# Three normed tiles of a linear-attention and SwiGLU kernel go from TensorE's transpose to the DMA's, and their gain to ScalarE

## Chip, cores and metric

The kernel runs on one core of a Trainium2 chip. The metric is device time in microseconds of one execution, lower is better. One further execution was profiled; its trace gives the span (first to last instruction of the program), and its own time contains a little more than the span.

## What is computed

The reference is an RWKV-6 recurrence followed by a gated feed-forward layer. Sizes: batch B = 4, H = 8 heads, S = 768 steps, D = 48 per head, so the model width is 384; the feed-forward width is 1536. All inputs are float32.

```python
for t in range(S):
    cur = einsum('bhd,bhe->bhde', u * k[t], v[t])
    y[t] = einsum('bhd,bhde->bhe', r[t], state + cur)
    state = w[t][..., None] * state + einsum('bhd,bhe->bhde', k[t], v[t])
x  = y.transpose(0, 2, 1, 3).reshape(3072, 384)
xn = x / sqrt(mean(x * x, -1) + 1e-6) * rms_g
g, val = xn @ w_gate, xn @ w_val
out = (g * sigmoid(g) * val) @ w_out
```

## The kernel before

The 768 steps are cut into six superblocks of 128. In names such as `xn_pe.2.0` the first number is the superblock and the second the batch; for `gate_mm`, `val_mm`, `silu` and `h_mul` the second number is one of twelve slices of the feed-forward width.

The recurrence of one superblock and batch is done in closed form. `ln` takes the logarithm of the decay, `cs_mm` sums it along the block on TensorE, `cs_add` adds the block's own step on VectorE, `exp_r` and `exp_k` take exponentials on ScalarE, and `r_mul` (VectorE) and `k_mul` (GpSimd from superblock 2 on) scale r and k by them into one tile `rk`. `rk_tr` transposes `rk`, by DMA from superblock 2 on. `q_mm` makes the scores, `q_mask_e`, `q_copy_o` and `q_mask_o` mask them, `y_mm` applies them and the old state, `st_mm` and `st_new` make the new state. `bonus_mul`, `bonus_sum` and `bonus_v` make the term with u, which `x_add` adds.

The norm of one tile of 128 rows and 384 columns: `x_sq` sums the squares on ScalarE, `x_rstd` makes the reciprocal root on GpSimd, `xn_mul` (L585) scales the rows on ScalarE into a bfloat16 tile `xn`, of which there are three buffers. The feed-forward matmuls need this tile with the 384 columns on partitions, in `xnt`, one tile of 128 x 3 x 512 for the four batches of a superblock, in two buffers. There are two ways to it:

- `xn_pe` (L596): three 128x128 transposes on TensorE into one PSUM bank; then `xn_out` (L607) multiplies by the norm's weights `gT` on VectorE while it copies from PSUM into `xnt`. Superblocks 0 to 3 go this way.
- `xn_tr` (L590): one DMA transpose issued by SP, from `xn` straight into `xnt`; then `xn_gain` multiplies `xnt` in place, one third of the columns of all four batches at a time. Superblocks 4 and 5 go this way.

```python
nc.sync.dma_start_transpose(xnt[n][:, :, j * L:(j + 1) * L], bank.pop(("xn", n, j)))
```

Then come 24 groups of matmuls a superblock (`gate_mm` and `val_mm`, three matmuls of 512 columns each), `silu` on ScalarE, `h_mul` on VectorE, and per batch `o_mm` (twelve matmuls), `o_out` (copy from PSUM, on VectorE or ScalarE) and `out_dma`.

The order is written out by hand. The string `ORDER` lists 1086 steps over all engines, and each step puts its instructions at the end of its engines' queues. An engine does its own instructions in that order and waits only for the data and the buffers that the next one needs. All loads, DMA transposes and stores of the output stand in SP's queue; the loads of the weights are issued by GpSimd. The feed-forward part of one superblock and the recurrence of the next are interleaved in `ORDER`.

PSUM has eight banks in three rings: "a" (names ps_au, ps_av) and "b" (ps_bu, ps_bv) are used by `cs_mm`, `cs_add`, `gate_mm` and `val_mm`, "q" (ps_qu, ps_qv, ps_qx, ps_qz) by the rest, `xn_pe` and `o_mm` among them. A helper looks ahead in `ORDER` for the last use of each bank and hands out the one that came free first.

Of the kernel before, what the change touches and what calls it, by code (L numbers as in the profile page):

```python
# [74 lines left out]
exp_k.3.3 cs_mm.3.2 xn_out.2.3 o_mm.1.2 load_r.3.2 k_mul.3.1 w_tot.3.3 rk_tr.3.0 r_mul.3.3 cs_add.3.2 out_dma.1.0
xn_out.2.1 load_v.3.0 exp_r.3.2 gate_mm.2.5 exp_k.3.2 r_mul.3.2 w_tot.3.2 val_mm.2.0 gate_mm.2.0 bonus_mul.3.0
bonus_mul.3.2 k_mul.3.2 o_out.1.3 bonus_sum.3.0 silu.2.5 rk_tr.3.1 load_k.3.3 o_out.1.2 q_mm.3.0 silu.2.0 q_mask_e.3.0
val_mm.2.1 bonus_v.3.0 h_mul.2.0 gate_mm.2.1 load_w.4.1 load_v.3.1 load_k.4.3 st_mm.3.2 k_mul.3.3 q_copy_o.3.0
silu.2.1 rk_tr.3.2 load_v.4.0 rk_tr.3.3 val_mm.2.5 gate_mm.2.11 load_k.4.0 bonus_sum.3.1 cast_v.3.0 out_dma.1.1
# [10 lines left out]
o_out.2.0 x_rstd.3.2 xn_mul.3.2 w_tot.4.0 ln.4.2 exp_r.4.1 load_r.5.1 x_rstd.3.3 k_mul.4.0 xn_out.3.0 load_r.4.3  # L90
out_dma.1.3 bonus_sum.4.1 xn_pe.3.1 xn_out.3.1 ln.4.3 exp_k.4.1 bonus_mul.4.2 xn_mul.3.3 r_mul.4.1 k_mul.4.1 w_tot.4.1
out_dma.2.0 o_mm.2.1 cs_mm.4.2 xn_pe.3.3 bonus_mul.4.0 cast_v.4.1 xn_pe.3.2 o_out.2.1 cs_mm.4.3 bonus_sum.4.2
rk_tr.4.0 xn_out.3.3 cs_add.4.3 load_k.5.3 o_mm.2.3 exp_r.4.3 xn_out.3.2 cs_add.4.2 bonus_mul.4.3 r_mul.4.3 w_tot.4.3
exp_k.4.3 exp_r.4.2 rk_tr.4.1 o_out.2.3 exp_k.4.2 load_v.4.2 val_mm.3.1 gate_mm.3.6 bonus_sum.4.0 k_mul.4.3 r_mul.4.2
st_mm.4.0 w_tot.4.2 load_r.5.3 load_k.5.0 val_mm.3.0 o_out.2.2 silu.3.6 st_new.4.0 k_mul.4.2 gate_mm.3.1 q_mm.4.0
cast_v.4.2 out_dma.2.2 bonus_sum.4.3 silu.3.1 gate_mm.3.0 q_copy_o.4.0 silu.3.0 h_mul.3.1 q_copy_o.4.1 gate_mm.3.3
val_mm.3.6 gate_mm.3.8 rk_tr.4.3 q_mask_e.4.0 h_mul.3.0 h_mul.3.6 st_mm.4.1 bonus_v.4.0 q_mask_e.4.1 q_mask_o.4.0
load_r.5.0 bonus_v.4.2 rk_tr.4.2 load_v.5.1 q_mask_o.4.1 bonus_v.4.1 silu.3.3 gate_mm.3.4 val_mm.3.4 val_mm.3.3
y_mm.4.0 silu.3.4 st_new.4.1 gate_mm.3.9 h_mul.3.4 load_v.4.3 load_r.5.2 load_k.5.1 silu.3.8 x_add.4.0 val_mm.3.8
# [5 lines left out]
load_v.5.3 x_sq.4.2 xn_tr.4.0 h_mul.3.11 x_sq.4.3 xn_tr.4.1 val_mm.3.5 st_mm.4.3 h_mul.3.5 x_rstd.4.2 cs_mm.5.1
cs_add.5.1 ln.5.2 xn_mul.4.2 x_rstd.4.3 o_mm.3.2 o_out.3.2 cs_mm.5.2 xn_tr.4.2 exp_k.5.1 cs_add.5.2 exp_r.5.1 o_mm.3.0
xn_mul.4.3 r_mul.5.1 ln.5.3 ln.5.0 xn_tr.4.3 cs_mm.5.0 st_new.4.3 exp_r.5.2 cast_v.5.3 exp_k.5.2 o_mm.3.1 out_dma.3.2
cs_add.5.0 out_dma.2.3 r_mul.5.2 exp_r.5.0 cs_mm.5.3 r_mul.5.0 st_mm.4.2 exp_k.5.0 cs_add.5.3 exp_r.5.3 o_mm.3.3
bonus_mul.5.1 xn_gain.4.0 xn_gain.4.2 xn_gain.4.1 k_mul.5.0 r_mul.5.3 exp_k.5.3 o_out.3.1 out_dma.2.1 o_out.3.0
gate_mm.4.0 val_mm.4.1 gate_mm.4.1 val_mm.4.0 bonus_sum.5.1 st_new.4.2 k_mul.5.1 k_mul.5.3 silu.4.0 load_v.5.0  # L110
rk_tr.5.0 silu.4.1 h_mul.4.0 gate_mm.4.3 gate_mm.4.2 rk_tr.5.1 silu.4.3 val_mm.4.2 bonus_sum.5.0 k_mul.5.2 gate_mm.4.4
silu.4.2 bonus_v.5.1 o_out.3.3 cast_v.5.0 h_mul.4.1 val_mm.4.3 q_mm.5.0 gate_mm.4.6 h_mul.4.2 bonus_mul.5.2 h_mul.4.3
silu.4.4 q_copy_o.5.0 q_mask_o.5.0 gate_mm.4.5 out_dma.3.1 q_mask_e.5.0 y_mm.5.0 silu.4.6 q_copy_o.5.1 bonus_v.5.0
rk_tr.5.2 load_v.5.2 silu.4.5 rk_tr.5.3 x_add.5.0 val_mm.4.4 q_mask_o.5.1 gate_mm.4.8 val_mm.4.5 q_mask_e.5.1
h_mul.4.4 bonus_sum.5.2 q_mm.5.2 q_copy_o.5.2 gate_mm.4.10 val_mm.4.6 bonus_v.5.3 cast_v.5.2 silu.4.8 h_mul.4.5
q_copy_o.5.3 cast_v.5.1 q_mask_e.5.3 q_mask_e.5.2 q_mask_o.5.2 silu.4.10 h_mul.4.6 gate_mm.4.7 x_sq.5.0 y_mm.5.1
q_mask_o.5.3 silu.4.7 bonus_v.5.2 x_rstd.5.0 x_add.5.1 val_mm.4.10 y_mm.5.3 val_mm.4.7 y_mm.5.2 gate_mm.4.11 x_add.5.3
x_sq.5.1 h_mul.4.10 x_sq.5.3 x_rstd.5.1 h_mul.4.7 xn_mul.5.1 val_mm.4.8 out_dma.3.3 gate_mm.4.9 silu.4.11 x_rstd.5.3
xn_mul.5.3 xn_tr.5.1 h_mul.4.8 xn_mul.5.0 val_mm.4.11 xn_tr.5.3 x_add.5.2 x_sq.5.2 x_rstd.5.2 val_mm.4.9 silu.4.9
# [5 lines left out]
val_mm.5.9 gate_mm.5.10 silu.5.9 h_mul.5.6 h_mul.5.9 val_mm.5.8 silu.5.10 val_mm.5.10 gate_mm.5.11 h_mul.5.8
h_mul.5.10 val_mm.5.11 silu.5.11 h_mul.5.11 o_mm.5.0 o_mm.5.3 o_out.5.3 o_mm.5.1 out_dma.5.3 o_out.5.1 o_out.5.0
out_dma.5.0 o_mm.5.2 out_dma.5.1 o_mm.5.4 o_out.5.2 out_dma.5.2 o_out.5.4 out_dma.5.4
# [597 lines left out]
```

## Time and profile before

| what | value |
|---|---|
| three runs | 200.31, 201.06, 201.94 us (median 201.06) |
| profiled execution | 200.28 us |
| its span | 198.6 us |
| TensorE matmul busy | 191.9 us (97%) |
| VectorE busy | 151.4 us (76%) |
| ScalarE busy | 137.3 us (69%) |
| GpSimd busy | 125.2 us (63%) |
| DMA traffic | 32.41 MB, mean 163 GB/s |
| granted TensorE clock | full in all 40 slices of the page |

Engines are named PE (TensorE matmul), PEld (its weight loads), DVE (VectorE), ACT (ScalarE), POOL (GpSimd) and SP (the queue that issues DMAs). In rows of the timeline the first number is the start in us from the beginning of the span, the second the length, then engine, line, operation, tile written and tiles read, shapes and the count of merged instructions; brackets tell how long the engine had been idle and who ended that. L235 is a helper for all activations that need a table (`ln`, `exp_r`, `exp_k`, `silu`), so there the tile names tell the step: lw is `ln`, ps_au or ps_av written in place is `exp_r`, ek is `exp_k`, sg is `silu`. Matmul records overlap, so the step from one start to the next is the time that a matmul holds TensorE.

### The profile page before, as it was taken

The page shows a single profiled execution, that of the slowest core. Times are in us where ns is not written, and L with a number is a line of the kernel's source. Part 1 is how long each engine was busy: PE and PEld are TensorE (multiplying, and loading weights), DVE is VectorE, ACT ScalarE, POOL GpSimd, SP SyncE. Part 2 cuts the span into 40 slices and gives each one's busy share as a digit, 9 for nine tenths or more (in the row PEclk, how much of TensorE's full clock was granted, in tenths as well). Part 3 has the DMA queues.
Part 4 walks back from the last instruction along what each step waited for, and adds up shares of the span by engine and source line. Part 5 has one row for each costly group of instructions (what it writes and reads, how often), then busy time and mean ns, then how long its engine had stood idle before and what let it go on. Part 6 is the DMA issues. An engine that isn't in the chain of part 4 may idle for free.

```text
span 198.6 us, 4409 instructions
## 1 busy us (share of the span) xinstructions
PE 191.9 (97%) x1577; PEld 113.9 (57%) x1577; DVE 151.4 (76%) x290; ACT 137.3 (69%) x279; POOL 125.2 (63%) x184
## 2 busy tenths in 40 slices
PE   7979998999999999999999999999999999999994
PEld 3556574465665565665556665556655565555562
DVE  6358989989998799987889989987887973173611
ACT  4399989579979569958559959399786683164300
POOL 5378993189399687899939899867686851000000
PEclk9999999999999999999999999999999999999999
DMA  6999999999999998999899879995499012032012
GB/s 153 268 235 176 183 220 203 214 180 211 179 195 224 206 196 196 236 198 207 193 195 225 188 171 204 204 183 107 138 187 208 0 25 60 6 112 83 0 59 101
DMA packets 121566, 32.41 MB, mean 163 GB/s; under 512 B 116420, under 2 KB 120392, under 8 KB 121544
## 3 DMA queue, kind: packets, MB, share of 16 engines
q1 hardware_dynamic: 119504, 28.58, 67.3%
q0 software_dynamic: 2032, 3.54, 10.0%
q8 instruction: 12, 0.20, 0.4%
q14 instruction: 10, 0.08, 0.1%
q10 hardware_dynamic: 8, 0.00, 0.0%
HBM read 25.96 MB, written 4.72 MB: 154 GB/s over the span
## 4 chain that ended last, share of the span: by engine, by line
PE 72%; SPq 18%; DMA 6%; POOL 2%; issue 1%; ACT 0%; POOLq 0%
SPq L248 16%; PE ps_av L626 10%; PE ps_bu L626 10%; PE ps_bv L626 10%; PE ps_au L626 10%; PE ps_qv L672 7%; PE ps_qz L672 7%; PE ps_qu L672 5%; PE ps_qx L672 4%; DMA wo_sb<-in_moe_w_out_dram 4%; DMA vt<-in_v_dram 3%; SPq L261 2%; PE ps_qz L502 1%; PE ps_qx L552 1%; PE ps_av L417 1%
## 5 line engine op out<-in xcount | busy, mean ns | idle before, releaser
L672 PEld LDWEIGHTS <-ht 128*128 128x128 bf16 x300 | 28.2, 98 | 17.0 <-issue 0.5
L626 PEld LDWEIGHTS <-wg_sb 128*128 128x128 bf16 x216 | 23.1, 114 | 19.7 <-DMA wg_sb<-in_moe_w_gate_dram 0.7
L626 PEld LDWEIGHTS <-wv_sb 128*128 128x128 bf16 x216 | 22.8, 114 | 19.0 <-DMA wv_sb<-in_moe_w_val_dram 1.0
L658 DVE TENSOR_TENSOR ht<-ps_bv,sg 128x512 bf16<-128x512 f32 x35 | 24.0, 686 | 10.1 <-PE ps_bv L626 9.2
L235 ACT ACTIVATE sg<-ps_av 128x512 bf16<-128x512 f32 x37 | 22.0, 595 | 12.3 <-PE ps_av L626 12.0
L626 PE MATMUL ps_av<-xnt,wg_sb 128*128 128x512 bf16 x111 | 30.1, 380 | 0.0
L626 PE MATMUL ps_bu<-xnt,wv_sb 128*128 128x512 bf16 x111 | 30.1, 380 | 0.0
L658 DVE TENSOR_TENSOR ht<-ps_bu,sg 128x512 bf16<-128x512 f32 x37 | 25.4, 686 | 6.0 <-PE ps_bu L626 5.2
L626 PE MATMUL ps_bv<-xnt,wv_sb 128*128 128x512 bf16 x105 | 28.5, 380 | 0.6 <-DMA wv_sb<-in_moe_w_val_dram 0.5
L626 PE MATMUL ps_au<-xnt,wg_sb 128*128 128x512 bf16 x105 | 28.5, 380 | 0.2 <-DMA wg_sb<-in_moe_w_gate_dram 0.2
L235 ACT ACTIVATE sg<-ps_au 128x512 bf16<-128x512 f32 x35 | 21.0, 599 | 10.8 <-PE ps_au L626 9.0
L467 POOL TENSOR_TENSOR ruk<-rt,kt 128x384 f32<-128x384 f32 x24 | 24.1, 1003 | 6.6 <-DMA kt<-in_k_dram 4.8
L468 POOL TENSOR_TENSOR ruk<-ruk,u_bc 128x384 f32<-128x384 f32 x24 | 24.4, 1017 | 1.9
L520 POOL TENSOR_SCALAR_AFFINE_SELECT qts<-qts 128x512 bf16<-128x512 bf16 x20 | 12.9, 653 | 15.1 <-ACT qts L513 14.6
L477 POOL TENSOR_TENSOR ydiag<-vt,diag 128x384 f32<-128x384 f32 x24 | 19.9, 833 | 1.0 <-DVE rk L461 0.5
L461 POOL TENSOR_TENSOR rk<-kt,ek 128x384 bf16<-128x384 f32 x16 | 15.9, 1007 | 2.3 <-ACT ek L235 2.3
L672 PE MATMUL ps_qv<-wo_sb,ht 128*128 128x384 bf16 (+1 forms) x96 | 15.0, 306 | 0.0
L672 PE MATMUL ps_qz<-wo_sb,ht 128*128 128x384 bf16 x84 | 14.8, 326 | 0.0
L233 ACT ACT_TABLE_LOAD x10 | 12.8, 1283 | 1.8 <-PEq L709 1.6
L235 ACT ACTIVATE lw<-wt 128x384 bf16<-128x384 f32 (+1 forms) x20 | 11.1, 578 | 4.2 <-DMA wt<-in_w_dram 4.1
L472 DVE TENSOR_REDUCE diag<-ruk 128x8 f32<-128x384 f32 x24 | 12.9, 543 | 0.7 <-POOL ruk L468 0.7
L585 ACT ACTIVATE xn<-xb,rstd 128x384 bf16<-128x384 f32 x20 | 11.8, 605 | 0.8 <-POOL rstd L580 0.8
(180 smaller groups left out, 373.6 us busy)
## 6 DMA issues: line engine op xcount, KB each, us to landing
rt<-in_r_dram SPq DMA_DIRECT2D x24, 192.0 KB, 3.9
kt<-in_k_dram SPq DMA_DIRECT2D x24, 192.0 KB, 4.0
vt<-in_v_dram SPq DMA_DIRECT2D x24, 192.0 KB, 3.7
out_dram<-ob SPq DMA_DIRECT2D x23, 192.0 KB, 2.3
wt<-in_w_dram SPq DMA_DIRECT2D x16, 192.0 KB, 4.0
wt<-in_w_dram SPq DMA_DIRECT2D x4, 384.0 KB, 4.4
wo_sb<-in_moe_w_out_dram POOLq DMA_DIRECT2D x3, 384.0 KB, 7.1
wg_sb<-in_moe_w_gate_dram POOLq DMA_DIRECT2D x1, 768.0 KB, 9.8
```

The source lines that it names most:

```text
L233: nc.scalar.preload_act_table_set(table_name)
L235: return nc.scalar.activation(**kw).ins
L248: dmas["load_" + which, n, j] = nc.sync.dma_start(out=inp[which, n, j], in_=t[j, :, n * L:(n + 1) * L, :].rearrange("h t d -> t h d")).ins
L461: eng.tensor_tensor(out=rk[:, n % 2, j, 1, :, 0:D], in0=inp["k", n, j], in1=bank["cs_k", n, j][:, 0:DM].rearrange("p (h d) -> p h d", h=H) ...
L467: nc.gpsimd.tensor_tensor(out=ruk[n, j], in0=inp["r", n, j], in1=inp["k", n, j], op=ALU.mult)
L468: nc.gpsimd.tensor_tensor(out=ruk[n, j], in0=ruk[n, j], in1=u_bc, op=ALU.mult)
L472: nc.vector.tensor_reduce(out=diag[n, j].rearrange("p h o -> p (h o)"), in_=ruk[n, j], axis=mybir.AxisListType.X, op=ALU.add)
L477: nc.gpsimd.tensor_tensor(out=ydiag[n, j], in0=inp["v", n, j], in1=diag[n, j].to_broadcast([128, H, D]), op=ALU.mult)
L520: nc.gpsimd.affine_select(out=qts[n, j][:, 1], in_=qts[n, j][:, 1], compare_op=ALU.is_gt, fill=0.0, base=0, pattern=[[0, NP], [1, 128]], c ...
L626: nc.tensor.matmul(ps[:, cols], lhsT=units(ws, c, f), rhs=xnt[n][:, c, cols], start=(first and c == 0), stop=(c == KC - 1))
L658: nc.vector.tensor_tensor(out=ht[n][:, f, :], in0=bank.pop(("v", n, f)), in1=bank.pop(("sg", n, f)), op=ALU.mult)
L672: nc.tensor.matmul(ps[:, cols], lhsT=ht[n][:, f, b * L:(b + 1) * L], rhs=wo_sb[:, f, cols], start=(f == 0), stop=(f == FC - 1))
```

## The change

Three of the 24 tiles, batch 0 of superblock 2 and batches 0 and 1 of superblock 3, go from the first way to a mixture of both: `xn_tr` transposes them by DMA, and `xn_out`, for these three, multiplies the three 128x128 blocks of `xnt` in place on ScalarE, with the weight as a scale per partition. Their `xn_pe` steps go. One load is moved up by a few steps. Nothing else in the program changes.

```diff
+    XT_DMA = sel("30 20 31")
...
     def xn_out(n, j):
         if n not in xnt:
             xnt[n] = pt.tile([128, KC, TS], BF16, name="xnt")
+        if (n, j) in XT_DMA:
+            for c in range(KC):
+                t = xnt[n][:, c, j * L:(j + 1) * L]
+                nc.scalar.activation(out=t, in_=t, func=AF.Copy, scale=gT[:, c:c + 1])
+            return
         ps = bank.pop(("xt", n, j))
```

The rest is in `ORDER`. Its lines are broken anew, so the diff is given here by steps, with neighbours:

```diff
 o_mm.1.0 cs_mm.3.1
-xn_pe.2.0
 exp_r.3.0 ln.3.2
...
 load_k.3.2 load_r.3.3
+load_r.3.2 xn_tr.2.0
 xn_pe.2.1
-xn_out.2.0
 exp_r.3.3 exp_k.3.3
+xn_out.2.0
 cs_mm.3.2 xn_out.2.3 o_mm.1.2
-load_r.3.2
 k_mul.3.1 w_tot.3.3 rk_tr.3.0
...
 cast_v.3.3 val_mm.2.11 xn_mul.3.0
+xn_tr.3.0
 q_mask_e.3.2
...
 cs_mm.4.1 x_sq.3.1
-xn_pe.3.0
 x_add.3.2
...
 x_rstd.3.3 k_mul.4.0
-xn_out.3.0
 load_r.4.3 out_dma.1.3
+xn_tr.3.1
 bonus_sum.4.1
-xn_pe.3.1 xn_out.3.1
 ln.4.3 exp_k.4.1 bonus_mul.4.2 xn_mul.3.3
+xn_out.3.0
 r_mul.4.1 k_mul.4.1 w_tot.4.1 out_dma.2.0 o_mm.2.1 cs_mm.4.2 xn_pe.3.3 bonus_mul.4.0 cast_v.4.1 xn_pe.3.2 o_out.2.1
+xn_out.3.1
 cs_mm.4.3 bonus_sum.4.2
```

Three PSUM banks of ring "q" fewer are taken, so some later `o_mm` and `xn_pe` steps get another bank of that ring.

More of the change, by code (lines that the diff above doesn't have):

```diff
@@ L75 @@
[L75 to L79, printed above, removed]
@@ L90 @@
[L90 to L94, printed above, removed]
@@ L95 @@
[L95 to L99, printed above, removed]
@@ L105 @@
[L105 to L109, printed above, removed]
@@ L110 @@
[L110 to L119, printed above, removed]
@@ L125 @@
[L125 to L127 removed]
+load_r.3.0 x_sq.2.2 xn_mul.2.0 cast_v.3.2 cs_add.3.0 x_add.2.3 exp_k.3.0 x_sq.2.3 o_mm.1.0 cs_mm.3.1 exp_r.3.0 ln.3.2
+x_rstd.2.2 o_mm.1.1 st_new.2.3 load_r.3.1 out_dma.0.3 w_tot.3.0 r_mul.3.0 xn_mul.2.1 k_mul.3.0 xn_mul.2.2 cs_add.3.1
@@ new lines @@
+exp_k.3.1 xn_pe.2.2 cs_mm.3.3 x_rstd.2.3 o_out.1.0 exp_r.3.1 bonus_mul.3.1 xn_out.2.2 xn_mul.2.3 o_mm.1.3 w_tot.3.1
+xn_pe.2.3 o_out.1.1 cs_add.3.3 r_mul.3.1 load_k.3.2 load_r.3.3 load_r.3.2 xn_tr.2.0 xn_pe.2.1 exp_r.3.3 exp_k.3.3
+xn_out.2.0 cs_mm.3.2 xn_out.2.3 o_mm.1.2 k_mul.3.1 w_tot.3.3 rk_tr.3.0 r_mul.3.3 cs_add.3.2 out_dma.1.0 xn_out.2.1
+load_v.3.0 exp_r.3.2 gate_mm.2.5 exp_k.3.2 r_mul.3.2 w_tot.3.2 val_mm.2.0 gate_mm.2.0 bonus_mul.3.0 bonus_mul.3.2
+k_mul.3.2 o_out.1.3 bonus_sum.3.0 silu.2.5 rk_tr.3.1 load_k.3.3 o_out.1.2 q_mm.3.0 silu.2.0 q_mask_e.3.0 val_mm.2.1
@@ new lines @@
+x_add.3.3 cs_mm.4.0 bonus_mul.4.1 ln.4.1 cs_mm.4.1 x_sq.3.1 x_add.3.2 x_sq.3.2 cs_add.4.0 h_mul.2.8 st_new.3.3
+o_mm.2.0 x_sq.3.3 o_mm.2.2 exp_r.4.0 load_k.4.2 cs_add.4.1 exp_k.4.0 r_mul.4.0 x_rstd.3.1 xn_mul.3.1 o_out.2.0
+x_rstd.3.2 xn_mul.3.2 w_tot.4.0 ln.4.2 exp_r.4.1 load_r.5.1 x_rstd.3.3 k_mul.4.0 load_r.4.3 out_dma.1.3 xn_tr.3.1
+bonus_sum.4.1 ln.4.3 exp_k.4.1 bonus_mul.4.2 xn_mul.3.3 xn_out.3.0 r_mul.4.1 k_mul.4.1 w_tot.4.1 out_dma.2.0 o_mm.2.1
+cs_mm.4.2 xn_pe.3.3 bonus_mul.4.0 cast_v.4.1 xn_pe.3.2 o_out.2.1 xn_out.3.1 cs_mm.4.3 bonus_sum.4.2 rk_tr.4.0
@@ new lines @@
+xn_out.3.3 cs_add.4.3 load_k.5.3 o_mm.2.3 exp_r.4.3 xn_out.3.2 cs_add.4.2 bonus_mul.4.3 r_mul.4.3 w_tot.4.3 exp_k.4.3
+exp_r.4.2 rk_tr.4.1 o_out.2.3 exp_k.4.2 load_v.4.2 val_mm.3.1 gate_mm.3.6 bonus_sum.4.0 k_mul.4.3 r_mul.4.2 st_mm.4.0
+w_tot.4.2 load_r.5.3 load_k.5.0 val_mm.3.0 o_out.2.2 silu.3.6 st_new.4.0 k_mul.4.2 gate_mm.3.1 q_mm.4.0 cast_v.4.2
+out_dma.2.2 bonus_sum.4.3 silu.3.1 gate_mm.3.0 q_copy_o.4.0 silu.3.0 h_mul.3.1 q_copy_o.4.1 gate_mm.3.3 val_mm.3.6
+gate_mm.3.8 rk_tr.4.3 q_mask_e.4.0 h_mul.3.0 h_mul.3.6 st_mm.4.1 bonus_v.4.0 q_mask_e.4.1 q_mask_o.4.0 load_r.5.0
```

62 lines of the change are left out of this document (39 added, 23 removed).

## The prediction

> **What bounds the kernel now.** I read the page first for the chain that ended last, then the windows for what TensorE does along that chain, then the timeline around the six places that the change touches.
>
> ```profile
> span 198.6 us, 4409 instructions
> ...
> PE 72%; SPq 18%; DMA 6%; POOL 2%; issue 1%; ACT 0%; POOLq 0%
> ```
>
> ```profile
> 82.84:86.60 3.76, 3.76 (x32) 2.40 (x30) 3.25 (x9) 3.62 (x9) 3.51 (x6) 1.00 1.05 190
> 53.00:196.00 143.00, 142.47 (x1115) 84.18 (x1114) 108.46 (x209) 95.33 (x196) 90.23 (x132) 1.00 0.68 149
> ```
>
> The second row (columns: stretch, its length, busy time of PE, PEld, DVE, ACT, POOL, granted clock, DMA share, GB/s) is the main reading. From 53 to 196 us TensorE works 142.47 of 143.00 us at full clock. The chain is queue and DMA at the beginning and TensorE from there on. The three moved tiles all lie inside this stretch (82 to 118 us). So a TensorE instruction taken out there shortens the kernel by its own share of the stream, and anything that makes TensorE wait lengthens it. VectorE time is worth nothing in itself. The first row shows that the DMA engines are full (share 1.05, overlapping packets counted) just where the first new DMA transpose is put.
>
> **The change, part by part.** The time around the span is 200.28 - 198.6 = 1.7 us, which no part touches. The profiled run is 0.8 us below the median of 201.06, so I make the sum against 200.28 and carry it to the median.
>
> *Removed from TensorE: 9 transposes (xn_pe.2.0, 3.0 and 3.1, three each).*
>
> ```profile
> 82.66 0.33 PE L596 MATMUL ps_qx<-ident,xn 128*128 128x128 bf16 x3
> 82.83 0.49 PE L672 MATMUL ps_qu<-wo_sb,ht 128*128 128x384 bf16 x2
> ```
>
> The three transposes start at 82.66 and the next matmul at 82.83: they hold the stream for 0.17 us, though their records last 0.33, since records overlap. All three steps stand in the same dense stream, so 3 x 0.17 = 0.50 us.
>
> *Removed from VectorE: three gain products of 0.55 us each* (the kind of the 89.00 row below). It is off the chain, so zero; it only lets VectorE come earlier to its next wait.
>
> *Added to the SP queue: three DMA transposes, one of them behind load_r.3.2, which moves up.* In the SP queue nothing stands between the old and the new place of load_r.3.2, so its own move costs nothing.
>
> ```profile
> L596 PE MATMUL ps_qu<-ident,xn x18: 218/219/219, 26.0 to 116.0; 128*128 128x128 bf16 x18
> ...
> L590 SPq DMA_TRANSPOSE xnt<-xn x8: 1178/1198/1390, 133.5 to 166.0; - x8
> ...
> DMA to landing us min/median/max: 2.3/2.3/3.1
> ```
>
> ```profile
> DMA to landing us min/median/max: 2.7/3.3/3.8
> ```
>
> The first fence is tile xn, the second the landings of tile rkT (16 larger transposes, mostly in the full DMA stage). The same instruction already runs for superblocks 4 and 5: 1.2 us of SP, landing 2.3 to 3.1 us after issue where DMA is half empty; rkT's took up to 3.8 us. I take 2.3 to 3.8 as the bounds, and 3.3 as the value, for the full stage.
>
> *Superblock 2.* SP first:
>
> ```profile
> 80.84 2.00 SPq L248 DMA_DIRECT2D rt<-in_r_dram  x2
> 83.90 1.36 SPq L489 DMA_TRANSPOSE rkT<-rk  x1
> ```
>
> ```profile
> 81.19 0.60 ACT L585 ACTIVATE xn<-xb,rstd 128x384 bf16<-128x384 f32 x1
> ```
>
> SP is free at 82.84 and would wait until 83.90 for rk. xn.2.0 is ready at 81.79, so xn_tr.2.0 issues at 82.84 and holds SP to 84.04: rk_tr.3.0 comes 0.14 us later, without a reader in a hurry (its q_mm stands behind the first two matmul groups of superblock 2). The landing is at 82.84 + 2.3 to 3.8 = 85.1 to 86.6.
>
> ```profile
> 86.73 0.48 ACT L235 ACTIVATE ek<-ps_bu 128x384 f32<-128x384 f32 x1
> 89.19 0.48 ACT L235 ACTIVATE ps_av<-ps_av 128x388 f32<-128x388 f32 x1 [1.97 <-DVE ps_bv L425]
> ```
>
> xn_out.2.0 now stands on ScalarE between these two (exp_k.3.3 and exp_r.3.2), in an idle time of 1.97 us. It is three products of 128 columns in place. Their price is not in the trace; the nearest rows:
>
> ```profile
> L612 ACT ACTIVATE xnt<-xnt,gT 128x512 bf16<-128x512 bf16 x1 | 0.7, 712 | 0.0
> ```
>
> The same product on 512 columns takes 712 ns, the 384-column scaling by rstd 610 ns (114.11 row below), so about 102 ns per 128 columns and about 400 ns for 128. Two scalings in a row start 0.5 us apart and last 0.6 (111.50 row), so 0.1 overlaps: 0.3 us each, 0.9 us per tile. Bounds: 0.6 (0.2 each, half of the extrapolated price) to 1.5 (no cheaper than a 384-column one, 0.5 each). All shifted by -0.17, ScalarE reaches the step at 87.0 and is done at 87.9, at worst 88.5; exp_r.3.2 is released at 89.0. Hidden; cover left 0.5 to 1.1 us. The first matmul of superblock 2 needs all four tiles:
>
> ```profile
> 89.00 0.55 DVE L607 TENSOR_TENSOR xnt<-ps_qu,gT 128x384 bf16<-128x384 bf16 x1
> ...
> 89.70 0.81 PE L626 MATMUL ps_au<-xnt,wg_sb 128*128 128x512 bf16 x3
> ```
>
> The last VectorE tile (xn_out.2.1) ends at 89.55, 0.15 before TensorE takes it. It hangs on TensorE's transposes of 2.3 and 2.1, so it moves up with them; the gain of 0.17 survives here.
>
> The xn tiles have three buffers, and a DMA read holds one for longer than TensorE did. xn_mul.2.3 comes before xn_tr.2.0 in the order, so it can only be given a tile whose reader stands ahead of it, which is 2.2's, read by TensorE. No wait on the DMA here; if there were one, the landing at 86.1 would hold xn_mul.2.3 by about 0.9 us, for which the 1.97 us of idle time would still serve.
>
> *Superblock 3.*
>
> ```profile
> 105.01 1.54 SPq L248 DMA_DIRECT2D rt<-in_r_dram  x1
> ...
> 105.58 0.61 ACT L585 ACTIVATE xn<-xb,rstd 128x384 bf16<-128x384 f32 x1
> ...
> 106.60 0.70 SPq L261 DMA_DIRECT2D wt<-in_w_dram  x1
> ```
>
> Here SP does wait. At 105.01 it issued load_r.4.2; now xn_tr.3.0 stands first and waits for xn_mul.3.0 (105.58 + 0.61 = 106.19), then issues for 1.2 us: load_r.4.2 and all loads behind it start up to 2.3 us later. The DMA queue drains meanwhile, so they then issue faster, and I take 1.1 us for their landings.
>
> ```profile
> wt<-in_w_dram SPq DMA_DIRECT2D x16, 192.0 KB, 4.0
> ...
> wo_sb<-in_moe_w_out_dram POOLq DMA_DIRECT2D x3, 384.0 KB, 7.1
> ```
>
> ```profile
> 111.50 1.10 ACT L585 ACTIVATE xn<-xb,rstd 128x384 bf16<-128x384 f32 x2
> 112.50 0.51 ACT L235 ACTIVATE lw<-wt 128x384 bf16<-128x384 f32 x1
> ...
> 114.11 0.61 ACT L585 ACTIVATE xn<-xb,rstd 128x384 bf16<-128x384 f32 x1
> 115.70 0.48 ACT L681 COPY ob<-ps_qv 128x384 f32<-128x384 f32 x1 [0.99 <-PE ps_qv L672]
> 117.21 0.48 ACT L235 ACTIVATE ps_av<-ps_av 128x388 f32<-128x388 f32 x1 [1.03 <-DVE ps_bv L425]
> 117.60 0.48 ACT L235 ACTIVATE ek<-ps_bv 128x384 f32<-128x384 f32 x1
> ```
>
> The tightest reader is ln.4.2 on ScalarE (112.50). Its load lands at 106.60 + 4.0 + 1.1 = 111.7, in time; at 2.3 it would be 112.9, 0.6 late. The next users (POOL's product of r and k) have about as much room.
>
> xn_out.3.0 comes behind xn_mul.3.3: 114.72 - 0.17 = 114.55 to 115.45. o_out.2.1 is released by TensorE at 115.70 - 0.50 = 115.20, so it goes at 115.45, 0.25 late, and ScalarE is free for the next start 0.42 later (exp spacing 117.21 to 117.60 is 0.39). xn_out.3.1 runs from 115.87 to 116.77. exp_r.4.3 could go at 117.21 - 0.50 = 116.71 and goes at 116.77; exp_k.4.3 ends 0.39 + 0.48 later, at 117.64.
>
> ```profile
> 118.31 0.81 PE L626 MATMUL ps_bv<-xnt,wv_sb 128*128 128x512 bf16 x3
> ```
>
> val_mm.3.1 writes the bank that exp_k.4.3 reads (ps_bv), and TensorE gets there at 118.31 - 0.50 = 117.81. It has 0.17 us to spare: the two idle times of 0.99 and 1.03 us hide the two products, but barely. At 1.5 us per tile, exp_k.4.3 would end at 118.84 and TensorE would lose 1.0 us. xn_tr.3.1 issues when xn_mul.3.1 is done, at 112.0, and lands at 115.3 (114.3 to 115.8), ahead of 115.87.
>
> **Sum:** -0.50 + 0 + 0 = -0.50 us: 199.8 in the profiled execution, 200.6 on the median's scale.
>
> A rule that speaks against this stands in the Trainium skill, VectorE: DVE Perf Modes, section The three transpose paths: 390 ns for a 128x128 transpose on TensorE, 1309 ns by DMA, and a DMA transpose only where TensorE's will not do. By it the nine would free 3.5 us of TensorE (an estimate from that page); the row's 0.17 us per three decides against that price, and the DMA's longer path agrees with the landings but runs beside the chain.
>
> **The rivals.**
>
> *ScalarE gives the gain back in superblock 3 (no change).* If the load stream holds SP until 113.2 and xn_tr.3.1 takes 3.8 us, it lands at 117.0; the product ends at 117.9, exp_k.4.3 at 118.77, and val_mm.3.1 starts 0.96 us late: -0.50 + 0.96 = +0.46, 201.5. For it: only 0.17 us of room. Against: both tiles have an idle time of their own.
>
> *A slow landing blocks ScalarE's queue (slower).* xn_out waits in order, so exponentials, output copies and SiLUs queue behind it. The places are xn_out.2.0, from a landing of 5.3 us on (89.02 - 0.9 - 82.84), and xn_out.3.1, from 3.9 (115.87 - 112.0). With the 7.1 us of wo_sb's loads (the longest median): 2.0 lands at 89.94, its product ends at 90.84 instead of the 89.70 at which the group began, +1.14; 3.1 lands at 119.1, its product ends at 120.0, exp_k.4.3 at 120.9, val_mm.3.1 comes 2.6 us after its 118.31. Together +3.7 us, 204.8. For it: DMA is full here, and a wait on ScalarE hits many readers. Against: of the 24 such transposes none that the trace follows took over 3.8 us.
>
> *TensorE frees the whole record.* If each transpose cost its 219 ns, 9 x 0.22 = 1.97 us go: 199.1. For it: only the records. Against: the start of the next matmul. The 390 ns of the Trainium skill (VectorE: DVE Perf Modes, The three transpose paths) would be the far end of this case, 197.6 as an estimate.
>
> *The change does nothing:* TensorE reaches another wait 0.5 us earlier, in the second half. 201.1. Against: 0.53 us of idle in 143.
>
> **How the numbers follow.** A measurement of this kernel can tell about 1% (2 us) from no change. Forecast 0.42, gain given back 0.27, slow landing 0.21, whole record 0.07, nothing 0.03. Over 1% faster: 0.05, of the whole record's. Over 1% slower: 0.21, the slow landing's with a little of the second. Within: 0.74. The low end, 199.4, is the forecast less a part of the whole-record case and the scatter between runs; the high end, 203.0, covers the given-back case with both upper bounds and the milder part of the slow landings, and leaves the rest out.
>
> **What would show it.** Right: gate_mm.2.5 starts near 89.5, val_mm.3.1 near 117.8, TensorE stays at 99% from 53 us to its end; xn_tr lands within 3.8 us; the idle times of 1.97, 0.99 and 1.03 us shrink. Wrong: ScalarE shows a wait for DMA xnt, TensorE one before val_mm.3.1 or for ScalarE's xnt, or ln.4.2 waits for wt.

## The result, and the profile after

The changed kernel takes 202.0 us (median of 19 runs, 200.4 to 203.7), the kernel before 200.84 us beside it (19 runs). The ratio is 1.0057, 95% interval 1.0033 to 1.0081: slower by 1.2 us, where 0.5 us faster was forecast. Both lie within the 1% that I had set as the bound, but the sign is wrong and the interval leaves no doubt of it. Executions in the slower state are left out of every ratio here: two of these 19 (203.71 us each), and up to four of twelve in the runs below (e4).

The page of the changed kernel: its span, and the shares of the chain that ended last.

```profile
span 200.9 us, 4381 instructions
...
PE 58%; DMA 17%; SPq 13%; ACT 5%; POOL 2%; issue 2%; DVE 2%; ACTq 0%; POOLq 0%
```

The same stretch as in the prediction, from the windows (length, then busy time of PE, PEld, DVE, ACT, POOL, granted clock, DMA share, GB/s):

```profile
53.00:196.00 143.00, 140.05 (x1077) 82.26 (x1092) 106.94 (x206) 97.75 (x204) 90.47 (x132) 1.00 0.71 150
```

TensorE was busy 142.47 us of this stretch and now is 140.05, at the same clock; the DMA share went from 0.68 to 0.71. (There are 1077 matmul records against 1115; nine fewer are the change's, and more are missing from this trace, so the busy time falls by more than TensorE really waits.) TensorE lost time twice. The timeline around the first place:

```profile
83.38 2.74 SPq L591 DMA_TRANSPOSE xnt<-xn  x1
...
85.19 2.11 PE L678 MATMUL ps_qv<-wo_sb,ht 128*128 128x384 bf16 x12
...
87.57 0.61 ACT L586 ACTIVATE xn<-xb,rstd 128x384 bf16<-128x384 f32 x1 [2.13 <-DMA xnt<-xn]
...
88.24 0.34 PE L597 MATMUL ps_qz<-ident,xn 128*128 128x128 bf16 x3 [0.94 <-ACT xn L586]
...
89.23 0.97 ACT L605 ACTIVATE xnt<-xnt,gT 128x128 bf16<-128x128 bf16 x3
...
90.80 0.81 PE L632 MATMUL ps_au<-xnt,wg_sb 128*128 128x512 bf16 x3
```

The third row is xn_mul.2.3. It waits 2.13 us for the DMA that reads xn.2.0 (first row: issue from 83.38 on, 2.74 us of SP, landed 4.1 us after the start of the issue). TensorE comes to xn_pe.2.3 and finds no xn: 0.94 us of idle time and 0.17 of the overlap that matmul records have in a dense stream, 1.11 us.

The second place, in superblock 3:

```profile
107.74 1.30 SPq L591 DMA_TRANSPOSE xnt<-xn  x1
...
114.59 2.08 SPq L591 DMA_TRANSPOSE xnt<-xn  x1
114.74 1.00 POOL L468 TENSOR_TENSOR ruk<-rt,kt 128x384 f32<-128x384 f32 x1 [0.51 <-DMA kt<-in_k_dram]
...
116.59 0.46 ACT L687 COPY ob<-ps_qv 128x384 f32<-128x384 f32 x1
116.85 0.55 DVE L473 TENSOR_REDUCE diag<-ruk 128x8 f32<-128x384 f32 x1 [1.70 <-POOL ruk L469]
...
117.78 0.55 DVE L426 TENSOR_TENSOR ps_bv<-ps_av,lw 128x384 f32<-128x384 f32 x1
118.39 0.99 ACT L605 ACTIVATE xnt<-xnt,gT 128x128 bf16<-128x128 bf16 x3 [1.34 <-DMA xnt<-xn]
119.28 0.47 ACT L236 ACTIVATE ps_av<-ps_av 128x388 f32<-128x388 f32 x1
119.69 0.47 ACT L236 ACTIVATE ek<-ps_bv 128x384 f32<-128x384 f32 x1
...
120.22 0.81 PE L632 MATMUL ps_bv<-xnt,wv_sb 128*128 128x512 bf16 x2 [0.99 <-ACT ek L236]
```

Two delays run side by side. xn_tr.3.1 issues at 114.59 and lands just before 118.39, so xn_out.3.1 holds ScalarE for 1.34 us, and exp_r.4.3 and exp_k.4.3 stand behind it. And a load of k, pushed back by xn_tr.3.0, holds GpSimd 0.51 us; VectorE's bonus_sum.4.2 waits 1.70 us for that product, and cs_add.4.3, which the same exponentials need, stands behind bonus_sum. TensorE waits before val_mm.3.1: 0.99 idle and 0.16 of overlap, 1.15 us.

In this execution it is the first delay that TensorE pays. cs_add.4.3 is done at 118.33 and ScalarE was free at 117.05; had the transpose landed by then, exp_r.4.3 could have started at about 118.4 in place of 119.28 (an estimate from these rows), and some 0.2 us of the 1.15 would be left. Nor is all of the 1.70 us the load's. The same instruction in the kernel before, and in e4 below, where GpSimd's product does not wait for k:

```profile
115.20 0.55 DVE L472 TENSOR_REDUCE diag<-ruk 128x8 f32<-128x384 f32 x1 [0.23 <-POOL ruk L468]
```

```profile
115.70 0.55 DVE L473 TENSOR_REDUCE diag<-ruk 128x8 f32<-128x384 f32 x1 [1.13 <-POOL ruk L469]
```

VectorE has lost two gain products of about 0.46 us ahead of it, so it comes earlier and waits longer; 1.13 us of wait are there without a late load.

I measure the kernel from here on by TensorE's stretch from the start of the last output group of superblock 0 to the end of its last matmul: 59.17 to 195.62 in the kernel before (136.45 us), 59.25 to 197.52 here (138.27). The +1.82 us is -0.50 + 1.11 + 1.15, with 0.06 over. That is more than the 1.2 us of the runs: this profiled execution took 202.65 us, 0.65 above its median, and before's was 0.56 below its own. What precedes the stretch changes from one execution to the next: in two traces of the same program it began at 58.88 and 59.89 (e5, e5b).

What follows the stretch is longer too. The last matmuls, first of the kernel before (its span ends at 198.6), then of the change (200.9):

```profile
194.47 1.15 PE L672 MATMUL ps_qv<-wo_sb,ht 128*128 128x192 bf16 x12
```

```profile
196.37 1.15 PE L678 MATMUL ps_qv<-wo_sb,ht 128*128 128x192 bf16 x12
```

From the end of the last matmul to the end of the span it takes 2.95 us before and 3.42 in the change. So this execution's +2.37 us is 0.08 ahead of the stretch, 1.82 in it and 0.47 behind it. The traces show the reason. At the end of the program SP waits for the eight semaphores that its DMAs take in turn, one after the other, 0.06 us from each to the next. In the kernel before, SP issues 141 DMAs, and the last store's semaphore is the last but one of this list; with one DMA more it is the last. With two or three more, however, it is the first or second, and the rest of the list comes after the store has landed. In e5 below (two more) the last of the eight waits comes 2.47 us after the last matmul, in the kernel before 2.05 us after it. All 20 traces agree with this; no run changes the order of the waits by itself.

### The profile page after: what moved, and what is told of

It is laid out like the page before. It is cut to its first block, busy times and chain, and to the rows that moved or that the text cites. A ratio compares the mean times of both kernels' runs of the same rounds, so it can differ in the third digit from the quotient of the medians.

```text
span 200.9 us, 4381 instructions
## 1 busy us (share of the span) xinstructions
PE 191.6 (95%) x1548; PEld 113.3 (56%) x1568; DVE 150.1 (75%) x287; ACT 139.8 (70%) x288; POOL 125.4 (62%) x184
## 4 chain that ended last, share of the span: by engine, by line
PE 58%; DMA 17%; SPq 13%; ACT 5%; POOL 2%; issue 2%; DVE 2%; ACTq 0%; POOLq 0%
SPq L249 10%; PE ps_av L632 10%; DMA kt<-in_k_dram 9%; PE ps_au L632 9%; PE ps_bu L632 9%; PE ps_bv L632 8%; PE ps_qx L678 4%; DMA xnt<-xn 4%; PE ps_qv L678 4%; PE ps_qu L678 4%; PE ps_qz L678 4%; DMA wo_sb<-in_moe_w_out_dram 4%; SPq L262 2%; ACT lw L236 1%; PE ps_qz L503 1%
## 5 line engine op out<-in xcount | busy, mean ns | idle before, releaser
L632 PE MATMUL ps_bu<-xnt,wv_sb 128*128 128x512 bf16 x101 | 29.0, 379 | 0.6
L678 PE MATMUL ps_qx<-wo_sb,ht 128*128 128x384 bf16 x84 | 14.9, 325 | 0.2 <-DMA wo_sb<-in_moe_w_out_dram 0.2
```

The source lines that it names most:

```text
L632: nc.tensor.matmul(ps[:, cols], lhsT=units(ws, c, f), rhs=xnt[n][:, c, cols], start=(first and c == 0), stop=(c == KC - 1))
L678: nc.tensor.matmul(ps[:, cols], lhsT=ht[n][:, f, b * L:(b + 1) * L], rhs=wo_sb[:, f, cols], start=(f == 0), stop=(f == FC - 1))
```

## The experiments

All ratios are to the kernel before on the same chip, with 95% intervals. "Four buffers" is this edit, made where an experiment needed it; the room comes from a buffer of `er`, the tiles of superblock 1's exponentials:

```diff
-        xn = bank["xn", n, j] = pt.tile([128, DM], BF16, name="xn", bufs=3)
+        xn = bank["xn", n, j] = pt.tile([128, DM], BF16, name="xn", bufs=4)
-             bank["cs_r", n, j] = small.tile([128, tot(n) + DM], FP32, name="er", bufs=NE)
+             bank["cs_r", n, j] = small.tile([128, tot(n) + DM], FP32, name="er", bufs=3)
```

| run | what it is | ratio | stretch, us against before | gaps of TensorE in it, us | behind it, us against before |
|---|---|---|---|---|---|
| after | the change | 1.0057 [1.0033, 1.0081] | +1.82 | 1.11 xn_pe.2.3; 1.15 val_mm.3.1 | +0.47 |
| e0 | before, four buffers | 1.0009 [0.9985, 1.0033] | +0.01 | none | +0.02 |
| e1 | change, four buffers | 1.0035 [1.0002, 1.0067] | +1.10 | 1.27 val_mm.3.1 | +0.48 |
| e2 | only 2.0 changed | 1.001 [0.9975, 1.0045] | +0.42 | 0.57 xn_pe.2.3 | +0.04 |
| e12 | only 2.0, four buffers | 0.9995 [0.9958, 1.0032] | -0.15 | none | -0.05 |
| e3 | only 3.0 and 3.1 | 1.0022 [0.999, 1.0054] | +0.68 | 1.01 val_mm.3.1 | +0.75 |
| e4 | e1, xn_tr.3.0 later | 1.0046 [1.0006, 1.0086] | -0.12 | 0.38 val_mm.3.1 | +0.45 |
| e4b | the same again | 1.0041 [1.0016, 1.0066] | +0.80 | 0.99 val_mm.3.1 | +0.67 |
| e5 | e4, 3.1 on TensorE | 1.0028 [1.0005, 1.005] | -0.32 | none | +0.42 |
| e5b | the same again | 1.004 [1.0011, 1.0068] | -0.33 | none | +0.47 |
| e6 | change, xn_tr.2.0 earlier | 1.0081 [1.0062, 1.01] | +0.94 | 1.17 val_mm.3.1 | +0.72 |
| e8 | before + ScalarE's products | 1.0009 [0.9987, 1.003] | +0.17 | none | +0.01 |
| e7 | before + three unread transposes | 1.006 [1.0027, 1.0093] | +1.30 | 1.16 val_mm.3.1 | +0.31 |
| e7b | the same again | 1.0064 [1.0037, 1.0092] | +0.03 | none | +0.33 |
| e14 | two of them, 2.0 and 3.0 | 1.0046 [1.0017, 1.0074] | +0.01 | none | +0.53 |
| e9 | 2.0, and 3.0 later | 1.0038 [1.0012, 1.0063] | +0.77 | 0.42 q_mm.4.0 | +0.67 |
| e13 | 3.0 alone | 0.9962 [0.9924, 0.9999] | +0.01 | none | +0.05 |
| e10 | e7 with one-row copies | 1.002 [0.9987, 1.0053] | +0.01 | none | +0.32 |
| e11 | e7 with whole-tile copies | 0.9998 [0.9967, 1.0029] | +0.02 | none | +0.31 |

The last three columns are of a single execution each, the ratio of many; where they differ (e5, e7b, e14), that is told below. The last column is the end of the program: near zero where SP has none or one DMA more, 0.31 to 0.75 us where it has two or three more, whether they transpose or only copy (e10, e11). In some of them the last store also lands later (2.40 us after the last matmul in e6, 1.97 before). The +0.17 of e8, and 0.16 of e9's +0.77, arise at 65.60 us, ahead of the first product or transpose that these runs add.

### The two waits

**e1**, the change with the edit above.

> The changed kernel with four xn buffers in place of three (the space is taken from a buffer of superblock 1's exponentials that is not waited for). Theory A, two separate waits: xn_mul.2.3 no longer waits for the DMA's read of xn.2.0, so TensorE's gap of 1.1 us before xn_pe.2.3 closes; the wait of ScalarE for xn_tr.3.1 (1.3 us) and TensorE's gap of 1.1 us before val_mm.3.1 stay. Some 0.7 to 1.1 us less than the changed kernel: ratio to before 1.000 to 1.003. Rival B, the extra DMA traffic makes everything late and the buffer does not matter: ratio stays at 1.005 to 1.006.

**e2** and **e3**, the change in one superblock alone, with three buffers.

```diff
-    XT_DMA = sel("30 20 31")
+    XT_DMA = sel("20")        # e2; e3: sel("30 31")
```

> Only batch 0 of superblock 2 goes by DMA; 3.0 and 3.1 as before. Theory A: the gap before xn_pe.2.3 is there (about 1.1 us, less 0.17 for the transposes taken out), none before val_mm.3.1: ratio 1.002 to 1.005. Rival C, the whole loss is made in superblock 3: ratio 0.999.

> Only 3.0 and 3.1 go by DMA; 2.0 as before. Theory A: xn_tr.3.0 holds SP and the loads behind it, xn_tr.3.1 issues about 2 us after xn_mul.3.1 is done and ScalarE waits for it; a gap of up to 1.1 us before val_mm.3.1, less 0.33 for the transposes: ratio 1.000 to 1.004. Rival D, the late xn_tr.3.1 is only a consequence of the stall in superblock 2: no gap, ratio 0.998.

**e0**, the kernel before with four buffers.

> Control: the kernel before, with only the buffers of e1 and e4 (four xn, three of superblock 1's exponentials). Nothing waits for either in the kernel before, so theory A expects no change: ratio 0.999 to 1.001, TensorE without a gap over 0.3 us from 53 us on. Rival F, the buffers themselves (other addresses, a wait in superblock 1) made e4 slower: ratio 1.003 or more.

**e6**, three buffers, xn_tr.2.0 ahead of the two loads of r:

```diff
-load_r.3.3 load_r.3.2 xn_tr.2.0
+xn_tr.2.0 load_r.3.3 load_r.3.2
```

> The changed kernel (three buffers) with xn_tr.2.0 ahead of load_r.3.3 and load_r.3.2 in SP's queue. Theory A with a first-in-first-out queue: xn_tr.2.0 issues at 82 us instead of 83.4 and has two loads fewer ahead of it, lands at 85 to 86 instead of 87.5; xn_mul.2.3 waits under 0.6 us instead of 2.1, the gap before xn_pe.2.3 is under 0.2 us; the gap before val_mm.3.1 stays: ratio 1.001 to 1.004. Rival H, a DMA transpose takes 4 us in this stage wherever it stands: landing 4 us after issue, gap 0.4 us or more.

**e12**, e2 with four buffers.

> Four buffers of xn and only tile 2.0 transposed by DMA with its product on ScalarE; 3.0 and 3.1 stay on TensorE. By the forecast's terms this keeps a gain of 0.17 us and meets no wait: 0.999 (0.997 to 1.001), TensorE's stretch 0.17 us shorter. If the load of this one transpose is enough: 1.002 to 1.004, with rk_tr.3.0 or a load behind it as the one that is late.

The first gap is the buffer's. It goes with four buffers (e1, e12), and it goes with three when the transpose reads xn.2.0 earlier; e6's timeline:

```profile
82.24 2.23 SPq L591 DMA_TRANSPOSE xnt<-xn  x1
...
85.67 0.61 ACT L586 ACTIVATE xn<-xb,rstd 128x384 bf16<-128x384 f32 x1
```

xn_mul.2.3 no longer waits. One buffer of `er` fewer costs nothing that can be measured (e0). The second gap is independent of the first, since e3 has it without any change in superblock 2. e1's timeline has the same pair of delays as the change:

```profile
115.87 0.55 DVE L473 TENSOR_REDUCE diag<-ruk 128x8 f32<-128x384 f32 x1 [1.54 <-POOL ruk L469]
...
117.66 0.98 ACT L605 ACTIVATE xnt<-xnt,gT 128x128 bf16<-128x128 bf16 x3 [1.44 <-DMA xnt<-xn]
```

But e6's time did not fall with the gap that it lost: 1.0081 in six runs, with an interval that overlaps the change's. Its profiled execution (202.38 us) adds up: 0.42 us more than before's ahead of the stretch, 0.94 in it and 0.72 behind it. I had taken the two waits for the whole loss.

### Taking the second wait away

**e4** and **e4b** (four buffers):

```diff
-xn_mul.3.0 xn_tr.3.0
+xn_mul.3.0
...
-load_r.4.3
+load_r.4.3 xn_tr.3.0
```

> Four xn buffers as in e1, and xn_tr.3.0 stands behind load_r.4.3 in SP's queue, so that SP does not wait for xn_mul.3.0 with the loads behind it. Theory A: xn_tr.3.1 issues at about 112 us and lands before ScalarE comes to it; neither gap is left; the 0.50 us of the nine transposes is gained: ratio 0.997 to 0.999. Rival E, the products on ScalarE themselves (2 x 0.97 us ahead of exp_k.4.3) make val_mm.3.1 late: the gap before val_mm.3.1 stays above 0.5 us, ratio 1.000 to 1.002.

> The kernel of e4 once more, since its times (ratio 1.0046) and its trace (TensorE's stretch from the last output matmul of superblock 0 to the end 0.1 us shorter than before) contradict each other. Theory A: one gap of 0 to 0.5 us before val_mm.3.1, none before xn_pe.2.3; ratio 0.998 to 1.002. Rival G, the position of xn_tr.3.0 behind the loads costs something that comes and goes: ratio again 1.003 or more, with a larger wait in the trace.

The loads come in time now, but xn_tr.3.1 still does not. In e4 it landed early enough to leave a gap of 0.38 us; in e4b, the same program, SP held it 2.2 us and the gap was 0.99. A smaller loss shows in e4b as well:

```profile
116.12 2.11 PE L678 MATMUL ps_qv<-wo_sb,ht 128*128 128x384 bf16 x12 [0.16 <-ACT ob L687]
```

This is o_mm.2.3. It takes the bank that o_out.2.1 copies on ScalarE, and o_out.2.1 stands behind the product xn_out.3.0. The loss, 0.2 to 0.3 us with the overlap, is in e1, e4b and e6, and is most of what their stretches lose beyond the gaps listed.

**e5** and **e5b**: the same with `XT_DMA = sel("20 30")`, so xn_pe.3.1 and VectorE's xn_out.3.1 come back.

> As e4, but 3.1 goes back to TensorE; 2.0 and 3.0 by DMA. Theory A: no wait is left at all, TensorE gains 2 x 0.17 = 0.33 us: no gap over 0.3 us from 53 us on, ratio 0.997 to 1.000. Rival E, the products on ScalarE cost by themselves: a gap before val_mm.3.1 of 0.2 us or more.

> The version with four buffers of xn, xn_tr.3.0 behind load_r.4.3 and tile 3.1 on TensorE once more, for a second time and a second trace. Theory A: 0.9985 (0.997 to 1.000), TensorE's stretch from the last output group of superblock 0 to its end 0.3 us shorter than before's. Rivals I and J: 1.002 to 1.004 again, and, if this trace falls into a slower execution than the first one did, a wait in it that the first trace did not show: for a load with I, behind a product of ScalarE with J.

```profile
53.00:195.00 142.00, 141.13 (x1093) 83.55 (x1107) 107.67 (x207) 96.73 (x200) 90.21 (x132) 1.00 0.71 151
```

There is no gap over 0.26 us in the stretch, and it is 0.32 and 0.33 us shorter, two tiles of 0.16: within the stretch exactly theory A. The runs say otherwise, twice: 1.0028 and 1.004. Part of that stands behind the stretch: the end is 0.42 and 0.47 us longer, which more than undoes the gain, so that stretch and end together are 0.10 and 0.14 us longer than before's. By the intervals the runs lose 0.1 to 1.0 us (e5) and 0.2 to 1.4 us (e5b). e5's trace is of its fastest execution (200.08 us; its median is 201.11). So more may be lost in most executions than these traces show.

### Each part as a load of its own

**e7** and **e7b**: the kernel before with four buffers, and the three DMA transposes issued besides into a tile nobody reads. **e14** leaves 3.1 out, **e13** leaves 2.0 and 3.1 out (and load_r.3.2 in its old place), **e9** has 2.0 and a later 3.0.

```diff
+    EXTRA = sel("20 30 31")   # e14, e9: sel("20 30"); e13: sel("30")
...
     def xn_tr(n, j):
+        if (n, j) in EXTRA:
+            nc.sync.dma_start_transpose(aside, kept[n, j])
+            return
```

**e8**: VectorE copies the three tiles without the weights, ScalarE multiplies in place at the change's places.

> The kernel before with four buffers of xn, and the three DMA transposes of the change issued besides at their places (load_r.3.2 moved up as in the change), into a tile that nobody reads; TensorE's transposes and VectorE's products all stay. What it adds is the transposes' load on SP and the DMA engines, with nobody waiting for their result. Theory A (the loss is the two waits): 1.000 (0.998 to 1.002), no gap of TensorE before xn_pe.2.3 or val_mm.3.1. Rival I (the transposes' traffic itself delays other loads in most executions): +0.5 to +1.0 us, 1.0025 to 1.005, with a reader of a load (ln.4.2, r_mul, k_mul or w_tot of superblock 3 or 4) later by that much.

> The same with only the two transposes that the version with 3.1 on TensorE has: xn_tr.2.0 at the change's place and xn_tr.3.0 behind load_r.4.3, again read by nobody. That version measured 1.0028 though its trace shows no wait; it saves 0.34 us of TensorE (two tiles of 0.17). Theory A: 1.000 (0.998 to 1.002). Rival I: 1.0028 plus 0.34 us, about 1.0045 (1.003 to 1.006). Rival J (the cost lies in ScalarE's products, not in the transposes): 1.000 here, and the cost in the run with the products alone.

> The kernel before with the product of tiles 2.0, 3.0 and 3.1 moved alone: TensorE transposes them as before, VectorE copies them out without the weights, and ScalarE multiplies in place at the places of the change; no DMA transpose is added. Theory A: the products lie in ScalarE's idle time, except that the one of 3.1 uses up the 0.17 us of room before val_mm.3.1: 1.000 to 1.0015 (0 to +0.3 us), trace without a new gap over 0.3 us. Rival J: +0.5 to +0.9 us, 1.0025 to 1.0045, as in the version with 3.1 on TensorE plus what that saves.

e8 costs nothing that can be measured. The products took what I had put down (tile xnt of e8, nine products of one 128x128 block each):

```profile
L616 ACT ACTIVATE xnt<-xnt,gT x9: 389/392/405, 87.5 to 117.1; 128x128 bf16<-128x128 bf16 x9
```

e7 costs as much as the whole change, with every transpose of TensorE still in place and no one waiting for the new ones. About 0.3 us of it is the end of the program. Its ten times fall into two groups, six from 200.84 to 201.25 us and four from 202.31 to 203.31. The profiled execution is of the second (203.21 us), and 1.3 us of it lie ahead of the stretch, before the first new transpose. Its timeline shows where the stretch lost time in that execution:

```profile
107.90 1.69 SPq L592 DMA_TRANSPOSE aside<-xn  x1
...
110.88 1.13 SPq L249 DMA_DIRECT2D kt<-in_k_dram  x1
...
116.24 1.00 POOL L470 TENSOR_TENSOR ruk<-rt,kt 128x384 f32<-128x384 f32 x1 [1.74 <-DMA kt<-in_k_dram]
...
118.34 0.55 DVE L475 TENSOR_REDUCE diag<-ruk 128x8 f32<-128x384 f32 x1 [2.04 <-POOL ruk L471]
...
119.28 0.56 DVE L428 TENSOR_TENSOR ps_bv<-ps_av,lw 128x384 f32<-128x384 f32 x1
...
119.87 0.48 ACT L236 ACTIVATE ps_av<-ps_av 128x388 f32<-128x388 f32 x1 [2.36 <-DVE ps_bv L428]
...
120.80 0.81 PE L632 MATMUL ps_bv<-xnt,wv_sb 128*128 128x512 bf16 x3 [0.99 <-DVE ps_bu L428]
```

Read it upward from TensorE: val_mm.3.1 needs the bank that exp_k.4.3 reads; the exponentials wait for cs_add.4.3; that stands on VectorE behind bonus_sum.4.2, which waits for GpSimd's product, which waits for load_k.4.2, which was issued behind xn_tr.3.0 and landed 5.2 us after its issue. (The row of val_mm.3.1 names cs_add.4.2, which ends within 0.03 us of exp_k.4.3.) No ScalarE product is in this chain. In e7b's execution (201.12 us) the same load came in time, and VectorE waited no longer than before:

```profile
115.71 0.55 DVE L475 TENSOR_REDUCE diag<-ruk 128x8 f32<-128x384 f32 x1 [0.22 <-POOL ruk L471]
```

In e9 another reader pays:

```profile
112.83 2.77 SPq L592 DMA_TRANSPOSE aside<-xn  x1
...
116.81 1.25 SPq L492 DMA_TRANSPOSE rkT<-rk  x1
...
122.41 0.23 PE L505 MATMUL ps_qz<-rkT 48*128 48x128 bf16 x1 [0.25 <-DMA rkT<-rk]
```

SP takes 2.77 us for the moved transpose, and rk_tr.4.0 behind it is late for q_mm.4.0 (a gap of 0.42 us in all).

### What in the transposes costs

**e10** and **e11**: e7 with plain copies in place of the transposes.

```diff
-            nc.sync.dma_start_transpose(aside, kept[n, j])
+            nc.sync.dma_start(out=aside[0:1], in_=kept[n, j][0:1].rearrange("p (c l) -> p c l", l=L))   # e10
+            nc.sync.dma_start(out=aside, in_=kept[n, j].rearrange("p (c l) -> p c l", l=L))             # e11
```

> The version with the extra transposes that nobody reads (it measured 1.006), but each transpose replaced by a copy of one row of the tile, 768 bytes: SP still waits in order for xn at the same three places, while the transfer itself is next to nothing. Theory K1 (the transposes' own work on SP and the DMA engines makes the loads late): 1.000 to 1.002, load_k.4.2 issued within 1 us of the kernel before, no gap before val_mm.3.1. Rival K2 (SP's wait in order for xn.3.0 is what makes the loads late): 1.003 to 1.006, with VectorE waiting for GpSimd's ruk ahead of cs_add.4.3 and a gap near 1 us before val_mm.3.1.

> The same with plain copies of the whole tile (128 rows of 768 bytes) in place of the transposes: the same bytes and the same places, without the transposing. If the bytes set the price (rival K3): 1.004 to 1.006, like the transposes. If the transposing does (K1): 1.000 to 1.002, with an SP issue near 0.6 us where the transposes took 1.2 to 2.7, and no gap before val_mm.3.1.

> Only the extra transpose of tile 3.0, at the change's place ahead of load_r.4.2, read by nobody; the others are left out. By the trace of the version with all three, the kt tile that GpSimd's product of 4.2 waits for comes 3 us late and holds VectorE's bonus_sum.4.2, behind which cs_add.4.3 stands. If this one transpose does that: 1.002 to 1.005, a gap of 0.4 to 1.2 us before val_mm.3.1, VectorE's wait for ruk over 1 us. If it takes all three: 1.000 to 1.0015, no gap over 0.3 us.

> The extra transposes of 2.0 and 3.0 at the change's places, read by nobody; 3.1's is left out. 3.0 alone put no gap in TensorE's stretch and measured no loss; all three measured 1.006 with a gap of 1.16 us. If the two add up on SP's queue (2.0 makes everything behind it late, so 3.0 finds the queue behind already): 1.003 to 1.006, load_k.4.2 landing 2.5 us or more later against its neighbours than in the kernel before, VectorE waiting for ruk over 1 us, a gap of 0.4 to 1.2 us before val_mm.3.1. If 3.1 was needed for it: 1.000 to 1.0015 and no gap over 0.3 us.

> The extra transposes of all three tiles, read by nobody, once more. If the price is the load's own: 1.004 to 1.008 again, and a gap before val_mm.3.1 again. If the first time was scatter (the runs with single transposes showed none): 1.000 to 1.003 and a stretch of TensorE as long as before's (136.5 us).

Tile `aside`, first of e7, then of e11 (issue time on SP, minimum, median and maximum in ns):

```profile
L592 SPq DMA_TRANSPOSE aside<-xn x3: 1183/1691/2482, 84.1 to 116.0; - x3
...
DMA to landing us min/median/max: 3.2/3.2/3.2
```

```profile
L592 SPq DMA_DIRECT2D aside<-xn x3: 471/1049/1211, 82.6 to 112.6; - x3
...
DMA to landing us min/median/max: 3.0/3.0/3.0
```

(The landing is that of the second of the three in each case; the trace does not follow the others.) The same bytes as plain copies cost nothing measurable: 0.9998, its upper end 1.0029 below the lower end of e7b, 1.0037, though not below that of e7, 1.0027. So the transposing costs, and the bytes alone do not. Whether by holding SP longer (median 1.69 us against 1.05) or by its work on the DMA engines, these runs do not separate. The order alone (e10, 1.002) can't be told from either. One transpose alone costs nothing measurable (e13, whose interval even lies just below 1, with nothing in its trace to speak for a gain; and e12 as a real change), two 1.0046, three 1.006 and 1.0064, so 3.1 is not needed for most of it; with intervals of 0.3% the step from two to three is not resolved. That the transposes add up on SP's queue would fit, but it is not shown: the end of the program makes a step at the same place, +0.05 us with one DMA more (e13), +0.53 with two (e14) and +0.31 and +0.33 with three (e7, e7b), and the copies have it too. My expectation for e14's trace failed: no gap, its execution being the fastest of that program (200.53). e7b's, too, had none, at 201.12 against a median of 201.57.

## Why the prediction was wrong

The forecast was -0.50 us and the runs say +1.2. By its own steps:

- **The term "Added to the SP queue", put at zero, is the main failure.** I priced each transpose by its readers and by 1.2 us of SP. e7 and e7b, which have only that term, measure +0.60% and +0.64%, or 1.2 to 1.3 us. Some 0.3 us of it is the end of the program, for which the forecast has no term and which any two or three DMAs bring. Of the rest the traces show one path: I gave load_k.4.2's readers "about as much room" as ln.4.2 and looked no further, and in e7 GpSimd's wait for kt (1.74 us), VectorE's for GpSimd (2.04 us against 0.23) and the order on VectorE carry the late load to TensorE. e7b's trace does not have this, so it is shown for one execution and not for the typical one. I also took 1.2 us of SP for each from a stage where the DMA was half empty, and the same instruction held SP for 1.30 to 2.74 us here.
- **"No wait on the DMA here" for xn_mul.2.3 was false.** It is given xn.2.0's buffer, whose transpose had not landed. I had said that a wait would be covered by ScalarE's 1.97 us of idle time, and that was false as well: TensorE's xn_pe.2.3 comes directly after xn_mul.2.3 and had no such cover. In its trace 1.11 us; in the times, the change less e1, 0.22% or 0.4 us, which the intervals only allow to be called likely.
- **xn_tr.3.1 "issues when xn_mul.3.1 is done, at 112.0, and lands at 115.3": the place was right, the time was not.** It issued at 114.59, behind the loads and a store that SP still had, and landed 3.8 us later. That is the rival "ScalarE gives the gain back in superblock 3", with a price of 1.15 us in place of 0.96. It was not the only cause: e5 has no such wait and is slower too. I had also let xn_out.3.0 make o_out.2.1 0.25 us late and not asked who takes its bank next: it is o_mm.2.3, which loses 0.2 to 0.3 us in e1, e4b and e6, though not in the change's own trace.
- **The gain of 0.17 us a tile was right.** The stretch of e12 is 0.15 us shorter for one tile, that of e5 and e5b 0.32 and 0.33 for two. The rival in which TensorE frees 219 ns a transpose is out.
- **ScalarE's product at 0.9 us a tile was right**: 0.97 to 0.99 us in the change, and hidden when alone (e8).
- **The landing of 2.3 to 3.8 us** was a little short: 4.1 us for 2.0, 3.0 for 3.0, 3.8 for 3.1. The slow landing of the second rival (7.1 us) did not come.
- Of "what would show it": gate_mm.2.5 came at 90.80 and not 89.5, val_mm.3.1 at 120.22 and not 117.8, and ScalarE waits for the DMA, which I had named as the signs that I was wrong.

The sums agree, though no run shows it by itself: +1.2 us of the transposes' load less 0.5 us of TensorE is +0.7 (e1, which has no buffer wait: 0.35%, 0.7 us), and +0.4 us for the buffer makes 1.1. That they come out may be partly luck. The wait on ScalarE, which sets val_mm.3.1 in the traces of the change and of e1, has no part in e7, where the late load sets it; the sum holds only if the one costs in most executions about what the other does, and that is not shown.

The rule of the Trainium skill that I weighed against the change (VectorE: DVE Perf Modes, Rules for kernel authors: TensorE for a 128x128 transpose if its result may go to PSUM, the DMA's transpose otherwise) gave the right sign for this kernel, though not by the nanoseconds of the table in the Trainium skill (VectorE: DVE Perf Modes, The three transpose paths): what decided were the waits on the transposes, their load on the queue, and the end of the program. In e5, e7b and e14 the profiled execution shows no loss from the start of the stretch on but that of the end (0.42, 0.33 and 0.53 us); in which instruction their other executions lose more is open. e7's trace shows one such place and e9's another.

## What to carry to other kernels

A DMA put into a queue that also carries loads is paid by whatever stands behind it, and the bill can arrive two engines away: follow each delayed load through its reader, and through what stands behind that reader on the reader's own engine. A buffer that a DMA reads is held until the landing, so name the instruction that gets it next and then the engine that waits for that instruction. And where waits come and go, price a suspected part by a kernel that has only this part, over many runs; the trace of one execution may be of one that was spared. Add a trace up over its whole span, too: here 0.3 to 0.7 us came behind the last matmul, which TensorE's stretch alone does not contain.

## What the hardware showed that I had not expected

- The same 128x384 transpose held SP for 1.18 us in a quiet stretch and for up to 2.94 us in a busy one (e1), and landed after 2.3 to 4.3 us. A plain copy of the same tile held it 0.5 to 1.2 us.
- Three unread transposes cost 1.2 us of the kernel, three plain copies of the same bytes nothing measurable.
- Two or three more DMAs of any kind on SP's queue made the end of the program 0.31 to 0.75 us longer, one more did not (0.05 us at most): the end waits for the queue's eight semaphores in a fixed order, and the number of DMAs decides where in that order the last one stands.
- In one and the same program xn_tr.3.1 held SP for 1.2 us in one execution and 2.2 in another (e4, e4b), and the gap on TensorE went from 0.38 to 0.99 us with it.
